# Attention and feed-forward on one core: other places of the row-maximum tiles among the key tiles

## The chip, the cores and the metric

The kernel runs on one core of a Trainium2 chip. The metric is the device time of one execution in microseconds (us). A core has TensorE (PE in the profile, with its weight loads as PEld), VectorE (DVE), ScalarE (ACT), GpSimd (POOL) and SyncE (SP), which here only issues DMAs. Each engine works through its own list of instructions in order.

## The reference

Attention over 8 batches of 8 heads, with 1152 keys of 64 numbers, and queries that are the means of two neighbours (576 of them), followed by a feed-forward layer over the 4608 rows that come out:

```python
q_pool = q.reshape(B, H, S // 2, 2, D).mean(axis=3)
scores = scale * np.matmul(q_pool, k.transpose(0, 1, 3, 2))
scores = scores - np.max(scores, axis=-1, keepdims=True)
attn = np.exp(scores)
attn = attn / (np.sum(attn, axis=-1, keepdims=True) + 1e-09)
out = np.matmul(attn, v)
...
h = x @ w_in
g = h - np.tanh(h)
return g @ w_out
```

## The kernel before

The attention part takes two heads at a time, a *pair*; there are 32 pairs (`n_pair`). The two heads of a pair lie on partitions 0 to 63 and 64 to 127, so their matmuls come in twos. A pair is worked in two halves of 288 queries (`HQ`). In a half, nine *key tiles* of 128 keys follow each other (`scores`): four products of two matmuls each, the query and key parts `hi` and `lo` against each other and one product of `ones_k` with `mb`, which subtracts the row maximum. They go into one PSUM tile `ps`; ScalarE takes the exponential of it into `p_f`. After the nine tiles `pv` multiplies all nine `p_f` with the values into one more `ps` tile (the product with the values), and after a pair's second half `z_sums` adds up the exponentials in the same tile. GpSimd prepares these sums (`z_part`).

The row maxima that `mb` holds have to be there before a pair begins. They are worked out for a later pair in between: `max_part` multiplies 128 queries with 384 keys, the `hi` parts alone, for both heads (two matmuls into one `ps` tile), and VectorE reduces the tile to maxima `mx`. There are 15 such products, called *maxima* here, for a pair (five groups of queries, three of keys). They stand in the second half of the pair two before it and in the first half of the pair just before it. When all 15 are there, `max_rows` reduces `mx` to `nm`, TensorE transposes it (`ps<-ident,nm`), ScalarE and VectorE split it into two parts `mt`, and DMAs bring them into `mb` by way of `m_dram`. The transposition opens a second half.

VectorE also makes `lo` of a coming pair and, in steps spread over the pairs, the split weights of the feed-forward layer (`w_block`, tiles `w`), and in seven of the second halves the reciprocals of a finished batch's sums (`rec`).

All `ps` tiles of the attention come from one pool `ps_a` of four buffers (two PSUM banks each): key tiles, maxima, the transposition, the product with the values. A new tile waits until the last read of the tile that had its buffer is done. Which buffer that is, the framework fixes when the program is built.

The order on every engine is that in which the Python code issues it (`InOrder`). The clock of that order is the unit `u`: a half has `G` = 18 units, a key tile is issued at every second one. `add(u, f, at=...)` puts a step into a table. Of a unit, table `first` runs before the key tile, then `early`, then the key tile, then `at`; `pv` comes at the end of a half's last unit. A maximum's reduction stands in `first` of the unit after the maximum. `spots`, in the loop over the pairs, holds the table and unit of the 15 maxima relative to the pair's own start: -54 opens the second half of the pair two before, -36 the first half of the pair before.

All of it is recorded under line 37 (`InOrder`), so the rows are told apart by their tiles.

Of the kernel before, what the change touches and what calls it, by code (L numbers as in the profile page):

```python
# [43 lines left out]
def kernel(  # L44
# [90 lines left out]
    t, n = chunks.pop()  # L135
# [4 lines left out]
    with ExitStack() as actx:  # L140
# [26 lines left out]
            nc.gpsimd.memset(ones_k[64 * h:64 * h + 2].bitcast(F32), 1.0)  # L167


        at, first, early = {}, {}, {}  # L170

        def banks(dtype=F32):
            return ps_a.tile([P, 2, 512], dtype, name="ps")
# [3 lines left out]
        def add(u, f, *args, at=at):  # L177
            at.setdefault(u, []).append(lambda: f(*args))
# [83 lines left out]
        def scores(w, half, kt, p):  # L262

            ks = slice(SQ + kt * P, SQ + (kt + 1) * P)
            qs = slice(half * HQ, (half + 1) * HQ)
            ps = banks()
            for i, (x, y) in enumerate(((w.hi[:, ks], w.hi[:, qs]), (w.hi[:, ks], w.lo[:, qs]), (w.lo[:, ks], w.hi[:, qs]),
                                        (ones_k, w.mb[:, qs]))):
                for h in range(2):
                    r = slice(64 * h, 64 * h + 64)  # L270
                    pe.matmul(ps[:, h, 0:HQ], x[r], y[r], start=(i == 0), stop=(i == 3))
            act.activation(p, ps[:, :, 0:HQ], AF.Exp, scale=1.0 / 16)
# [12 lines left out]
        def pv(u, hf):  # L285

            w, ps = hf.w, banks()
            hf.o = ps[:, 0]
            for kt in range(KT):
                for h in range(2):  # L290
                    pe.matmul(hf.o[64 * h:64 * h + 64, 0:HQ], w.v[:, h, kt], hf.p[kt][:, h], start=(kt == 0),
                              stop=(kt == KT - 1), tile_position=(0, 64 * h))
            add(u + 1, o_out, w, hf, at=first)
            w.halves.append(hf)
            if hf.n == 1:
                z_sums(u, w, ps[:, 1])
# [95 lines left out]
        for i, blk in enumerate(blocks):  # L392
            u = U * (i - 2) + 5 if i else 23
# [23 lines left out]
        for pi in range(n_pair):  # L417
            u = pi * U
            units = dict(load=-80, query_sums=-62, hi=-55, lo=-37, load_v=-30)
            row, steps = -19, (5, 11)  # L420

            spots = [x for half, us in ((-54, (2, 4, 8, 10, 12, 14, 16)), (-36, (2, 4, 8, 10, 14, 16)))
                     for x in [(early, half)] + [(at, half + i) for i in us]]
            if pi == 0:
                units.update(load=-70, query_sums=-62, hi=-60, lo=-41, load_v=-40)
                spots = [(at, -60 + i) for i in range(15)]
                row, steps = -43, (3, 4)
            if pi == 1:
                units.update(load=-104)
            add(u + units["load"], load, pi)  # L430
            add(u + units["query_sums"], query_sums, pi, dve if pi < 1 else pool)
            for c in range(0, KQ, SQ):
                add(u + units["hi"], hi_part, pi, c, c + SQ)
            add(u + units["lo"], lo_part, pi)
            for i, (when, x) in enumerate(spots):
                add(u + x, max_part, u + x, pi, i // 3, i % 3, at=when)
            add(u + units["load_v"], load_v, pi)
            add(u + row, max_rows, u + row, pi, steps)

        def run(u, at=at):  # L440

            while at.get(u):
                at[u].pop(0)()

        for u in range(min(at), 0):
            run(u, first)
            run(u, early)
            run(u)
        z_groups = {kts[-1]: kts for kts in ((0, 1, 2), (3, 4, 5), (6, 7))}
        for u in range(end + 60):  # L450
            run(u, first)
            run(u, early)
            n, r = divmod(u, G)
            if u < end and r % 2 == 0:
                if r == 0:
                    hf = Half()
                    hf.w, hf.n, hf.p, hf.zs = pairs[n // 2], n % 2, [], []
                hf.p.append(pf.tile([P, 2, HQ], F32, name="p_f"))
                scores(hf.w, hf.n, r // 2, hf.p[-1])
                if r // 2 in z_groups:  # L460
                    add(u + 1, z_part, hf, z_groups[r // 2])
            run(u)
            if u < end and r == G - 1:
                pv(u, hf)
        assert not any(x for t in (at, first, early) for x in t.values())


    wt = ctx.enter_context(tc.tile_pool(name="wt", bufs=1))
# [141 lines left out]
```

## Time and profile before

| | |
|---|---|
| time, median of 3 runs | 1665.53 us (1661.75 to 1668.51) |
| the profiled execution, its own time | 1668.33 us |
| its span in the profile | 1666.5 us |
| PE busy | 1621.7 us (97%) |
| DVE busy | 1322.2 us (79%) |
| ACT busy | 1021.2 us (61%) |
| POOL busy | 939.8 us (56%) |
| chain that ended last, by engine | PE 84%, DVE 13%, ACT 2%, issue 1% |

A row of a timeline names an engine's instructions merged where they are alike: start, time, and how many (x4 is two of a maximum and two of the key tile behind it). TensorE's matmuls overlap, so the starts tell more than the busy times. A wait stands in brackets with the instruction that ended it.

### The profile page before, as it was taken

What the parts mean: (1) busy time and instruction counts of PE and PEld (TensorE: products, weight loads), DVE (VectorE), ACT (ScalarE), POOL (GpSimd) and SP (SyncE); (2) the same over time, 40 slices, a digit from 0 to 9 for tenths busy, and PEclk for the clock granted to TensorE, in tenths of its full rate; (3) what the DMA queues carried; (4) which work ended last, traced back from release to release, by engine and by line L of the source; (5) the groups of instructions that cost most, each with busy time, mean ns of one, the idle gap of its engine ahead of it and who ended that gap; (6) DMA issues with size and microseconds to landing.
All of it is one profiled execution on the core that took longest, in us unless ns stands there. A gap on an engine that the chain in (4) does not pass through costs nothing.

```text
span 1666.5 us, 32223 instructions
## 1 busy us (share of the span) xinstructions
PE 1621.7 (97%) x12576; PEld 1251.9 (75%) x12576; DVE 1322.2 (79%) x1725; ACT 1021.2 (61%) x1865; POOL 939.8 (56%) x694
## 2 busy tenths in 40 slices
PE   5999999999999999999999999999999999999999
PEld 3666776777777677777778787887878787878897
DVE  7888889889888889888657677676767676776886
ACT  2655655656656556556566666566666666665776
POOL 2777878778778778778844243334334332422332
PEclk9999999999999999999999999999999999999999
DMA  3343443443344334335464101101010111010000
GB/s 139 118 136 107 139 136 108 126 134 122 124 128 130 124 115 144 123 106 163 143 242 158 38 26 40 37 14 51 26 51 26 38 39 38 26 37 15 25 27 26
DMA packets 72665, 147.86 MB, mean 89 GB/s; under 512 B 11136, under 2 KB 36672, under 8 KB 72512
## 3 DMA queue, kind: packets, MB, share of 16 engines
q1 hardware_dynamic: 72512, 145.80, 26.8%
q8 instruction: 99, 1.62, 0.4%
q14 instruction: 54, 0.44, 0.1%
HBM read 109.49 MB, written 36.27 MB: 87 GB/s over the span
## 4 chain that ended last, share of the span: by engine, by line
PE 84%; DVE 13%; ACT 2%; issue 1%; DMA 0%; DVEq 0%; ACTq 0%
PE ps L37 37%; PE ps_h L37 24%; PE ps_o L37 23%; DVE w L37 6%; DVE mx L37 6%; DVE nm L37 0%; DVE lo L37 0%; ACT g_s L512 0%; ACT g_m L513 0%; ACT g_s L511 0%; ACT g_u L509 0%; DMA q_n<-in_q_dram 0%; ACT g_hi L520 0%; ACT o_s L539 0%; ACT g_t L510 0%
## 5 line engine op out<-in xcount | busy, mean ns | idle before, releaser
L37 DVE TENSOR_REDUCE mx<-ps 128x2 f32<-128x768 f32 x480 | 434.3, 950 | 74.8 <-PE ps L37 74.7
L37 POOL TENSOR_TENSOR g_lo<-g_s,g_hi 128x512 fp32r<-128x512 f32 (+1 forms) x160 | 189.9, 1187 | 511.5 <-ACT g_hi L520 464.9
L37 ACT ACTIVATE p_f<-ps 128x576 f32<-128x576 f32 x576 | 361.5, 650 | 94.3 <-PE ps L37 79.7
L37 POOL TENSOR_TENSOR z<-p_f 128x576 f32<-128x576 f32 x192 | 279.6, 1456 | 154.7 <-ACT p_f L37 154.7
L37 PE MATMUL ps<-hi 64*128 64x288 f32 (+1 forms) x2112 | 316.9, 352 | 23.7 <-DVE mx L37 13.7
L37 PE MATMUL ps_h<-x,wi 128*128 128x512 f32 (+1 forms) x1440 | 327.2, 377 | 0.0
L37 PE MATMUL ps_o<-wo,g_hi 128*128 128x512 f32 x1008 | 311.6, 390 | 0.0
L37 PEld LDWEIGHTS ps_h<-x,wi 128*128 128x128 f32 x1440 | 260.0, 193 | 53.1
L37 PE MATMUL ps<-p_f,v 128*64 128x288 f32 x2304 | 293.5, 409 | 0.0
L37 PEld LDWEIGHTS ps<-hi 64*128 64x128 f32 x2112 | 194.6, 187 | 89.2 <-DVE mx L37 34.6
L509 ACT ACTIVATE g_u<-ps_h 128x512 f32<-128x512 f32 (+1 forms) x160 | 88.8, 555 | 267.8 <-PE ps_h L37 267.5
L37 PEld LDWEIGHTS ps<-p_f,v 128*64 128x64 f32 x2304 | 159.7, 137 | 113.7 <-ACT p_f L37 12.0
L514 DVE SCALAR_TENSOR_TENSOR ps_w<-g_u,ps_h 128x512 f32<-128x512 f32 (+1 forms) x160 | 102.9, 643 | 178.7 <-ACT g_t L510 177.0
L37 PEld LDWEIGHTS ps_o<-wo,g_hi 128*128 128x128 f32 x1008 | 187.5, 188 | 39.1
L37 POOL TENSOR_TENSOR z<-z,p_f 128x576 f32<-128x576 f32 x128 | 194.0, 1516 | 11.9 <-ACT p_f L37 2.0
L37 PE MATMUL ps_o<-wo,g_lo 128*128 128x512 f32 x504 | 196.3, 389 | 0.0
L37 PE MATMUL ps<-lo,hi 64*128 64x288 f32 x1152 | 171.0, 293 | 0.0
L37 PE MATMUL ps<-hi,lo 64*128 64x288 f32 x1152 | 170.9, 293 | 0.0
L37 PE MATMUL ps<-mb,ones_k 64*128 64x288 f32 x1152 | 170.3, 292 | 0.0
L37 ACT ACTIVATE o_s<-ps 128x288 f32<-128x288 f32 x64 | 26.3, 411 | 230.3 <-PE ps L37 230.3
L519 DVE COPY_PREDICATED g_s<-g_m,g_t 128x512 f32<-128x512 int32 (+1 forms) x160 | 116.2, 726 | 17.1 <-DVE g_s L518 0.9
L517 DVE SCALAR_TENSOR_TENSOR ps_w<-g_s,ps_w 128x512 f32<-128x512 f32 (+1 forms) x160 | 102.9, 643 | 16.6 <-ACT g_m L513 0.5
(68 smaller groups left out, 2398.9 us busy)
## 6 DMA issues: line engine op xcount, KB each, us to landing
q_n<-in_q_dram SPq DMA_DIRECT2D x32, 576.0 KB
kq<-in_k_dram SPq DMA_DIRECT2D x32, 576.0 KB
v<-in_v_dram SPq DMA_DIRECT2D x32, 576.0 KB
x_dram<-o_s SPq DMA_DIRECT2D x32, 288.0 KB
out_dram<-o_s SPq DMA_DIRECT2D x34, 256.0 KB
w_raw<-in_moe_w_in_dram SPq DMA_DIRECT2D x16, 512.0 KB
wi_dram<-w_hl SPq DMA_DIRECT2D x16, 512.0 KB
w_raw<-in_moe_w_out_dram SPq DMA_DIRECT2D x16, 512.0 KB
```

The source lines that it names most:

```text
L37: ins = self.tc.keep_in_program_order(f(*args, **kwargs))
L509: nc.scalar.activation(u, h, AF.Square)
L514: nc.vector.scalar_tensor_tensor(w, u, -P0, h, op0=ALU.add, op1=ALU.mult)
L517: nc.vector.scalar_tensor_tensor(w, s2, P2, w, op0=ALU.add, op1=ALU.mult)
L519: last = nc.vector.copy_predicated(s1, m.bitcast(I32), th).ins
```

## The change

The places of the 15 maxima change. Before, the half at -54 has one maximum in front of its first key tile (table `early`) and others behind key tiles 1, 2, 4, 5, 6, 7 and 8 (units 2, 4, 8, 10, 12, 14, 16); the half at -36 has one in front and six behind tiles 1, 2, 4, 5, 7 and 8. After, no maximum stands in front of a first key tile. The half at -54 has its eight behind tiles 1, 2, 4, 5, 7, and three behind 8, the half at -36 its seven behind 0, 1, 3, 4, 6 and two behind 8. The table `early` is gone. Pair 0's maxima keep their places.

```diff
-            spots = [x for half, us in ((-54, (2, 4, 8, 10, 12, 14, 16)), (-36, (2, 4, 8, 10, 14, 16)))
-                     for x in [(early, half)] + [(at, half + i) for i in us]]
+            spots = [half + i for half, us in ((-54, (2, 4, 8, 10, 14, 16, 16, 16)), (-36, (0, 2, 6, 8, 12, 16, 16))) for i in us]
...
-            for i, (when, x) in enumerate(spots):
-                add(u + x, max_part, u + x, pi, i // 3, i % 3, at=when)
+            for i, x in enumerate(spots):
+                add(u + x, max_part, u + x, pi, i // 3, i % 3)
...
             run(u, first)
-            run(u, early)
```

TensorE at the start of a second half (of a pair in the middle), before. The names are those of the words above, with the buffers' numbers; a maximum has 384 columns, a product of a key tile 288:

```order
L37 MATMUL ps_8029<-ident_60,nm_7994 10x128
L37 MATMUL ps_8033<-hi_7945 128x384 x2
L37 MATMUL ps_8037<-hi_7189 128x288 x2
L37 MATMUL ps_8037<-lo_7190,hi_7189 128x288 x2
L37 MATMUL ps_8037<-hi_7189,lo_7190 128x288 x2
L37 MATMUL ps_8037<-mb0_116,ones_k_118 128x288 x2
L37 MATMUL ps_8052<-hi_7189 128x288 x2
L37 MATMUL ps_8052<-lo_7190,hi_7189 128x288 x2
L37 MATMUL ps_8052<-hi_7189,lo_7190 128x288 x2
L37 MATMUL ps_8052<-mb0_116,ones_k_118 128x288 x2
L37 MATMUL ps_8062<-hi_7945 128x384 x2
```

and after:

```order
L37 MATMUL ps_8029<-ident_60,nm_7994 10x128
L37 MATMUL ps_8034<-hi_7186 128x288 x2
L37 MATMUL ps_8034<-lo_7187,hi_7186 128x288 x2
L37 MATMUL ps_8034<-hi_7186,lo_7187 128x288 x2
L37 MATMUL ps_8034<-mb0_116,ones_k_118 128x288 x2
L37 MATMUL ps_8048<-hi_7186 128x288 x2
L37 MATMUL ps_8048<-lo_7187,hi_7186 128x288 x2
L37 MATMUL ps_8048<-hi_7186,lo_7187 128x288 x2
L37 MATMUL ps_8048<-mb0_116,ones_k_118 128x288 x2
L37 MATMUL ps_8058<-hi_7942 128x384 x2
```

The maximum `ps<-hi 128x384` has left the place between the transposition and the first key tile; the first one now stands behind two key tiles.

TensorE at the end of the same half, the last key tile and what follows it up to the product with the values (`p_f,v`), before:

```order
L37 MATMUL ps_8171<-hi_7189 128x288 x2
L37 MATMUL ps_8171<-lo_7190,hi_7189 128x288 x2
L37 MATMUL ps_8171<-hi_7189,lo_7190 128x288 x2
L37 MATMUL ps_8171<-mb0_116,ones_k_118 128x288 x2
L37 MATMUL ps_8181<-hi_7945 128x384 x2
L37 MATMUL ps_8189<-p_f_8036,v_7532 64x288 x2
```

and after:

```order
L37 MATMUL ps_8163<-hi_7186 128x288 x2
L37 MATMUL ps_8163<-lo_7187,hi_7186 128x288 x2
L37 MATMUL ps_8163<-hi_7186,lo_7187 128x288 x2
L37 MATMUL ps_8163<-mb0_116,ones_k_118 128x288 x2
L37 MATMUL ps_8173<-hi_7942 128x384 x2
L37 MATMUL ps_8176<-hi_7942 128x384 x2
L37 MATMUL ps_8179<-hi_7942 128x384 x2
L37 MATMUL ps_8189<-p_f_8033,v_7531 64x288 x2
```

Three maxima stand between the last key tile and the product with the values, where there was one.

VectorE at the start of the same half, with the reciprocals that seven of the halves have, before:

```order
L37 TENSOR_SCALAR rec_7911<-rec_7911 128x36
L37 RECIPROCAL rec_7911<-rec_7911 128x36
L37 TENSOR_REDUCE mx_7944<-ps_8033 128x2
L37 TENSOR_TENSOR mt_7996<-ps_8029,mt_7996 10x128
L37 TENSOR_REDUCE mx_7944<-ps_8062 128x2
```

and after:

```order
L37 TENSOR_SCALAR rec_7910<-rec_7910 128x36
L37 RECIPROCAL rec_7910<-rec_7910 128x36
L37 TENSOR_TENSOR mt_7996<-ps_8029,mt_7996 10x128
L37 TENSOR_REDUCE mx_7941<-ps_8058 128x2
L37 TENSOR_REDUCE mx_7941<-ps_8074 128x2
```

The first reduction to `mx` stood ahead of `mt`, VectorE's part of the transposed maxima, and now stands behind it. On ScalarE and GpSimd the order of the instructions is the same.

## Rows read from the trace of the kernel before

**Rows 1.** One stretch: us; busy PE, PEld, DVE, ACT, POOL; granted clock, DMA share, GB/s.
```profile
110.00:805.00 695.00, 689.74 (x7663) 497.93 (x7661) 615.97 (x643) 418.37 (x738) 551.66 (x356) 1.00 0.39 127
```

**Rows 2.** Waits, 110 to 805 us: waiting, released by, total us, times, longest.
```profile
PEld ps L37 <- ACT p_f L37: 23.7, 126, 0.5
...
PEld ps L37 <- DVE mx L37: 15.9, 54, 0.8
```

**Rows 3.** Timeline of PE, a turn half: start, us, instruction, count.
```profile
506.42 0.28 PE L37 MATMUL ps<-ident,nm 128*10 128x128 f32 x1
506.62 0.57 PE L37 MATMUL ps<-hi 64*128 64x384 f32 x4
...
508.19 0.63 PE L37 MATMUL ps<-hi 64*128 64x384 f32 x4
...
509.05 0.46 PE L37 MATMUL ps<-hi 64*128 64x384 f32 x4
...
509.74 0.40 PE L37 MATMUL ps<-hi 64*128 64x288 f32 x2
...
512.85 0.51 PE L37 MATMUL ps<-hi 64*128 64x384 f32 x4
...
513.88 0.46 PE L37 MATMUL ps<-p_f,v 128*64 128x288 f32 x2
```

**Rows 4.** Timeline of DVE, the same half and the start of the next.
```profile
507.19 0.94 DVE L37 TENSOR_REDUCE mx<-ps 128x2 f32<-128x768 f32 x1
508.54 0.28 DVE L37 TENSOR_TENSOR mt<-ps,mt 10x128 fp32r<-10x128 f32 x1 [0.41 <-ACT mt L37]
508.75 1.80 DVE L37 TENSOR_REDUCE mx<-ps 128x2 f32<-128x768 f32 x2
510.76 4.42 DVE L37 TENSOR_REDUCE mx<-ps 128x2 f32<-128x768 f32 x5 [0.21 <-PE ps L37]
515.10 3.01 DVE L37 TENSOR_TENSOR lo<-kq,hi 128x1728 fp32r<-128x1728 f32 x1
...
520.96 0.96 DVE L37 TENSOR_REDUCE mx<-ps 128x2 f32<-128x768 f32 x1 [0.97 <-PE ps L37]
```

**Rows 5.** Timeline of ACT, the same half.
```profile
507.71 0.65 ACT L37 ACTIVATE p_f<-ps 128x576 f32<-128x576 f32 x1 [0.77 <-PE ps L37]
508.26 0.25 ACT L37 ACTIVATE mt<-ps 10x128 fp32r<-10x128 f32 x1
...
513.12 1.39 ACT L37 ACTIVATE p_f<-ps 128x576 f32<-128x576 f32 x2 [0.21 <-PE ps L37]
```

**Rows 6.** Timeline of PE, the plain half that follows: its first matmuls, the product.
```profile
520.47 0.58 PE L37 MATMUL ps<-hi 64*128 64x384 f32 x4
...
527.14 0.46 PE L37 MATMUL ps<-p_f,v 128*64 128x288 f32 x2
```

**Rows 7.** Timeline of PE, first key tiles of a half without maxima.
```profile
810.94 0.40 PE L37 MATMUL ps<-hi 64*128 64x288 f32 x2
...
811.58 0.29 PE L37 MATMUL ps<-hi 64*128 64x288 f32 x2
...
812.12 0.29 PE L37 MATMUL ps<-hi 64*128 64x288 f32 x2
```

**Rows 8.** Timeline of ACT, the first exponential there.
```profile
811.87 0.65 ACT L37 ACTIVATE p_f<-ps 128x576 f32<-128x576 f32 x1 [0.61 <-PE ps L37]
```

**Rows 9.** Timeline of PE, a turn half with reciprocals: transposition and product.
```profile
556.91 0.28 PE L37 MATMUL ps<-ident,nm 128*10 128x128 f32 x1
...
564.76 0.46 PE L37 MATMUL ps<-p_f,v 128*64 128x288 f32 x2
```

**Rows 10.** Timeline of PE, the long waits of three early halves.
```profile
75.67 0.58 PE L37 MATMUL ps<-hi 64*128 64x384 f32 x4 [1.83 <-DVE mx L37]
...
90.67 0.40 PE L37 MATMUL ps<-hi 64*128 64x288 f32 x2 [1.10 <-DVE mx L37]
...
102.75 0.58 PE L37 MATMUL ps<-hi 64*128 64x384 f32 x4 [0.84 <-DVE mx L37]
```

More of the change, by code (lines that the diff above doesn't have):

```diff
@@ L167 @@
             nc.gpsimd.memset(ones_k[64 * h:64 * h + 2].bitcast(F32), 1.0)
-        at, first, early = {}, {}, {}
+        at, first = {}, {}
         def banks(dtype=F32):
@@ L420 @@
             row, steps = -19, (5, 11)
-            spots = [x for half, us in ((-54, (2, 4, 8, 10, 12, 14, 16)), (-36, (2, 4, 8, 10, 14, 16)))
-                     for x in [(early, half)] + [(at, half + i) for i in us]]
+            spots = [half + i for half, us in ((-54, (2, 4, 8, 10, 14, 16, 16, 16)), (-36, (0, 2, 6, 8, 12, 16, 16))) for i in us]
             if pi == 0:
                 units.update(load=-70, query_sums=-62, hi=-60, lo=-41, load_v=-40)
-                spots = [(at, -60 + i) for i in range(15)]
+                spots = [-60 + i for i in range(15)]
                 row, steps = -43, (3, 4)
@@ L451 @@
             run(u, first)
-            run(u, early)
             n, r = divmod(u, G)
@@ L464 @@
                 pv(u, hf)
-        assert not any(x for t in (at, first, early) for x in t.values())
+        assert not any(x for t in (at, first) for x in t.values())
     wt = ctx.enter_context(tc.tile_pool(name="wt", bufs=1))
```

## The prediction

> **What bounds the kernel now.** I read the totals by stretch first, then the waits of the stretch in which the change works, and there single halves, instruction by instruction. From 110 to 805 us TensorE is busy for 689.7 of 695 us, at a granted clock of 1.00 [rows 1]. So only TensorE's own waits can give or take time, and they are small: its weight loads waited 23.7 us for exponentials (p_f) and 15.9 us for reductions (mx) [rows 2]. What these cost the totals don't tell; the starts of the instructions do.
>
> A **turn half** is the second half of a pair: it opens with the transposition of the row maxima (ps<-ident,nm) and has eight maxima among nine key tiles, 0 to 8. It takes 7.46 us from the transposition (506.42) to the first product with the values (513.88) [rows 3]. A **plain half**, the first of a pair, has seven and takes 6.67 us, 520.47 to 527.14 [rows 6]. The product with the values and the sums that follow are untouched.
>
> The prices. Key tiles follow each other in 0.53 us (811.58 to 812.12), but a tile that starts cold, first in a half or after a wait, takes 0.64 (810.94 to 811.58) [rows 7]. A maximum and a warm tile take 0.69 (509.05 to 509.74), so the maximum 0.16; where the maximum had waited, the two take 0.86 (508.19 to 509.05) [rows 3]. An exponential lasts 0.65 us and the next instruction of ACT follows 0.55 later (507.71 to 508.26) [rows 5]. It begins 0.93 after a cold tile (810.94 to 811.87) [rows 7, 8] and 0.84 after a warm one: tile 8 stands 0.17 behind the maximum of 512.85, at 513.02, and its exponential at 513.86 (513.12 + 1.39 - 0.65) [rows 3, 5]. A reduction lasts 0.94 and the next follows after 0.87 (five in 4.42) [rows 4]. A tile that waits for a buffer starts 0.05 after the read that frees it (508.75 + 0.94 = 509.69, tile at 509.74 [rows 3, 4]), the product with the values 0.11 after it (513.12 + 0.65 = 513.77, product at 513.88 [rows 3, 5]).
>
> All tiles share four PSUM buffers, and the built program fixes which read each tile waits for. Now reductions pace a turn half: the first runs at 507.19, in time in which VectorE would otherwise wait for the transposed maxima (mt at 508.54), and from 508.75 to 515.10 they run nearly without a gap [rows 4].
>
> **The change, part by part.** No instruction is added or removed. In 30 turn halves and 31 plain ones (the last three halves have no maxima) one maximum leaves the front, and two or three now stand behind tile 8.
>
> *The turn half*, from the transposition as zero. Tile 0 starts at 0.20, as the maximum did (506.42 to 506.62 [rows 3]), but cold, tile 1 at 0.84. Exponential 0 runs from 1.13 to 1.78. The first maximum stands at 1.37. Tile 2 needs exponential 0's buffer: 1.83, where TensorE was free at 1.53, so it has waited 0.3 and is cold. Second maximum 2.47, tiles 3 and 4 2.64 and 3.17, third maximum 3.70. On VectorE the early reduction is gone, and mt comes first. ACT turns the maxima 0.55 after exponential 0 began, at 1.68; VectorE's mt follows 0.28 later (508.26 to 508.54), at 1.96, the first reduction 0.21 after that (508.54 to 508.75 [rows 4, 5]), at 2.17, the second from 3.04 to 3.98. Tile 5 needs the second's buffer: 4.03, where TensorE was free at 3.86. It is cold again: fourth maximum 4.67, tiles 6 and 7 4.83 and 5.36, fifth maximum 5.89, tile 8 6.05. The three maxima behind it are covered, since the product with the values now takes tile 8's buffer and so waits for the last exponential, where it waited for the one before: 6.05 + 0.84 + 0.65 + 0.11 = 7.65; I take 7.66. Against 7.46 that is **+0.20 us, 30 times, +6.0**. What the change gains, that VectorE drains three reductions under the 6.6 us of product and sums (513.88 to 520.47 [rows 3, 6]), is there, but the latencies of the first and of the last exponential come out into the open.
> Bounds: with no wait but that for exponential 0, tile 8 stands 0.17 + 0.11 earlier: -0.08. If the two waits for reductions (tile 5's, and the last maximum's, which takes the fifth's buffer) each pass another 0.1 on: +0.40. I stay with the walk, whose prices are all from such halves.
>
> *The plain half*, from its first matmul as zero. Tile 0 at 0, its exponential 0.93 to 1.58; first maximum 0.64, tile 1 0.80, second maximum 1.37. Tile 2 waits for exponential 0 until 1.63. Tile 3 2.27, third maximum 2.80, tile 4 2.97, fourth 3.54; tile 5 waits 0.1 for exponential 3: 3.79. Tile 6 4.43, fifth 4.96, tile 7 5.13, tile 8 and two maxima until 6.5; the product waits for exponential 7 (5.95 to 6.60): 6.71. Against 6.67 that is **+0.04, 31 times, +1.2**. Bounds: -0.10 without tile 5's wait and with the product right behind the maxima, +0.15 if the last maximum's wait for a reduction ends last.
>
> *The reciprocals.* In seven turn halves VectorE also adds and inverts the sums of a finished batch ahead of the first reduction, and the half takes 7.85 us (556.91 to 564.76 [rows 9]) instead of 7.46. After the change mt stands behind them, for which VectorE has to wait anyway (0.41 us [rows 4]), so they are hidden: 7 x 0.39 = **-2.7**. This cover is thin: the plain half's last reductions end, by the walk, some 0.4 us later than now, and with them the steps on the weights (w) that stand ahead of mt. They reach 1.2 us after the transposition (now 507.19 - 506.42 = 0.8 at the latest [rows 3, 4]), 0.7 ahead of mt, 0.1 with the reciprocal. Uncovered, it gives back these 2.7 us and no more.
>
> *The start.* In three halves of the first 110 us VectorE comes late from more such steps, and TensorE waits 1.83, 1.10 and 0.84 us [rows 10]. Now it has up to two more tiles and a maximum to do, 1.2 us, before it meets a late reduction, and no more can be saved than these waits exceed the usual 0.3. I estimate 1.0, 0.5 and 0.5: **-2.0** (bounds -3.3 and 0).
>
> *Other queues.* ACT's and GpSimd's orders stay as they are, and no DMA of SP is moved. lo and w behind the turn half's reductions start some 0.8 us later; VectorE idles 0.97 us before the plain half's first reduction [rows 4], and that now comes later too, so nobody waits for them. Were that cover gone, the price would be in the plain half's +0.15.
>
> **Sum:** 6.0 + 1.2 - 2.7 - 2.0 = +2.5 us. The profiled execution took 1668.3 us, 0.2% over the median of 1665.5, so a difference this small may stand on the median: **1668.0 us**. A measurement of this kernel can tell about 0.5% (8.3 us) from no change; this is less.
>
> **A rule against it.** TensorE waited 1.83 us in one place, and waits of tenths stand in every half, at a granted clock of 1.00 [rows 1, 10]. The Trainium skill, page "TensorE: Matmul & The Clock Gate", section "A second HAM failure mode: psum-queue depth-cycling", says that short idle times between groups of matmuls, while the PSUM buffers are cycled, can make the clock swing between its levels and cost throughput. By that rule more waits per half speak against the change; the trace of before shows nothing of it. As a mechanism here, nine key tiles at half the clock add 9 x 0.53 = 4.8 us to each half that it hits, 290 us if all 61.
>
> **Rivals.** *Slower: the late first reduction.* In the turn half everything from tile 5 on hangs on mt, now ahead of all reductions, and on exponential 0 before it. With +0.40 and +0.15, and the reciprocals then uncovered: 30 x 0.40 + 31 x 0.15 - 2.0 = +14.7, 1680 us. It decides from +0.39 in a turn half on (30 x 0.39 + 1.2 - 4.7 = 8.2). For it: each of these waits ends right where a tile needs it. Against it: VectorE is free 0.7 us before mt. *Faster: the waits vanish.* With the lower bounds of both halves and of the start, 30 x (-0.08) - 31 x 0.10 - 2.7 - 3.3 = -11.5, 1654 us. For it: VectorE gets work under the product with the values. Against it: tile 2 must wait for exponential 0 whatever else happens. *The change does nothing:* the built program shows the maxima moved, so only the effect can be nil, which is the forecast. *The clock*, as above.
>
> **How the numbers follow.** Forecast, within 0.5%: 0.68. Slower by the late reduction 0.19, by the clock 0.01. Faster 0.12. The range takes in most of the faster case, down to 1656, and goes up to 1678, which leaves out the clock and about half of the slower case: below 0.2 in all. Faster 0.12, same 0.68, slower 0.20.
>
> **What would show it.** From the transposition to the values 7.66 us in a turn half, and 6.71 in a plain one; a wait for p_f ahead of the third key tile in both, a wait for mx ahead of the sixth in the turn half; the values' product released by the last exponential there; two to three reductions under it; halves with a reciprocal as long as the others. I am wrong if a turn half takes less than 7.4 or more than 7.85 us, or if the product or the sums, held here at their length, change.

## The result

| | before | after |
|---|---|---|
| time, median of 15 runs each | 1667.31 us (1661.75 to 1668.51) | 1670.91 us (1667.90 to 1672.67) |
| ratio to before, with its 95% interval | | 1.0023 [1.0015, 1.0031] |
| span of the profiled execution | 1666.5 us | 1669.7 us |
| turn half, transposition to the product with the values (median of 20) | 7.47 us | 7.71 us |
| turn half with reciprocals (median of 7) | 7.86 us | 7.71 us |
| plain half, first matmul to the product (median of 28) | 6.665 us | 6.70 us |

No change by the bound of 0.5%, and a small loss that the interval separates from zero: 0.0023 x 1665.5 = 3.8 us (2.5 to 5.2). The halves in this table and below are those that start behind 105 us, so that the three early ones of [rows 10] stand by themselves.

The page of after, its head, the busy times of TensorE and VectorE, and the chain that ended last by engine:

```profile
span 1669.7 us, 32193 instructions
...
PE 1629.6 (98%) x12576; PEld 1251.4 (75%) x12576; DVE 1287.9 (77%) x1725; ACT 1018.2 (61%) x1865; POOL 887.4 (53%) x694
...
PE 94%; ACT 3%; DVE 2%; issue 0%; DMA 0%; ACTq 0%; DVEq 0%
```

The same instructions, and VectorE is off the chain: it held 13% of it before. The stretch 110 to 805 us of after, with the columns of [rows 1]:

```profile
110.00:805.00 695.00, 691.40 (x7607) 493.84 (x7605) 580.00 (x640) 412.74 (x733) 498.50 (x353) 1.00 0.39 126
```

The granted clock is 1.00 as in [rows 1]. VectorE is 36 us less busy and GpSimd 53 us, with nearly the same instructions in the stretch; the last section comes back to that. The waits of the stretch, which answer to [rows 2]:

```profile
PEld ps L37 <- ACT p_f L37: 37.1, 163, 0.7
...
DVE mt L37 <- ACT mt L37: 19.3, 27, 0.9
PEld ps L37 <- DVE mx L37: 10.8, 54, 0.2
```

TensorE's waits have gone over from reductions (15.9 to 10.8 us) to exponentials (23.7 to 37.1 us), as a kernel shows in which the latencies of ScalarE lie open. For `mt` VectorE now waits in all 27 turn halves (8.4 us in 21 of them before).

TensorE in a turn half of after, which answers to [rows 3]. A row of [rows 3] takes in a maximum and the key tile behind it; here key tiles 0, 2, 5 and 8 (288 columns), the last maximum (384) and the product are shown apart:

```profile
507.26 0.28 PE L37 MATMUL ps<-ident,nm 128*10 128x128 f32 x1
507.47 0.40 PE L37 MATMUL ps<-hi 64*128 64x288 f32 x2
...
509.10 0.41 PE L37 MATMUL ps<-hi 64*128 64x288 f32 x2
...
511.29 0.40 PE L37 MATMUL ps<-hi 64*128 64x288 f32 x2
...
513.38 0.35 PE L37 MATMUL ps<-hi 64*128 64x288 f32 x2
...
514.60 0.45 PE L37 MATMUL ps<-hi 64*128 64x384 f32 x2
514.97 0.46 PE L37 MATMUL ps<-p_f,v 128*64 128x288 f32 x2
```

VectorE in the same half ([rows 4]):

```profile
509.23 0.28 DVE L37 TENSOR_TENSOR mt<-ps,mt 10x128 fp32r<-10x128 f32 x1 [0.83 <-ACT mt L37]
509.43 1.80 DVE L37 TENSOR_REDUCE mx<-ps 128x2 f32<-128x768 f32 x2
511.44 1.82 DVE L37 TENSOR_REDUCE mx<-ps 128x2 f32<-128x768 f32 x2 [0.21 <-PE ps L37]
513.58 3.55 DVE L37 TENSOR_REDUCE mx<-ps 128x2 f32<-128x768 f32 x4 [0.32 <-PE ps L37]
517.05 2.96 DVE L37 TENSOR_TENSOR lo<-kq,hi 128x1728 fp32r<-128x1728 f32 x1
```

ScalarE in the same half ([rows 5]):

```profile
508.40 0.65 ACT L37 ACTIVATE p_f<-ps 128x576 f32<-128x576 f32 x1 [0.61 <-PE ps L37]
508.94 0.25 ACT L37 ACTIVATE mt<-ps 10x128 fp32r<-10x128 f32 x1
...
512.19 2.69 ACT L37 ACTIVATE p_f<-ps 128x576 f32<-128x576 f32 x4 [0.21 <-PE ps L37]
```

Three places are to be seen. Tile 2 starts at 509.10, where exponential 0 has ended at 509.05 (508.40 + 0.65). Tile 5 starts at 511.29, behind the second reduction, which ended at 511.23 (509.43 + 1.80). The product with the values starts at 514.97, behind the last exponential, which ended at 514.88 (512.19 + 2.69), but also 0.37 behind the last maximum. That one starts at 514.60, 0.06 behind the end of a reduction (the first of the four from 513.58; 514.54). Which of the two holds the product these rows don't decide; e3 below bears on it. Before, the first reduction ran 0.77 us behind the transposition [rows 3, 4], now it runs 2.17 behind it. Two of the four reductions from 513.58 on start under the product.

The plain half that follows, first matmul, third key tile and product ([rows 6]), a turn half with reciprocals ([rows 9]), with VectorE in it, and TensorE's one wait that is left of [rows 10]:

```profile
521.56 0.40 PE L37 MATMUL ps<-hi 64*128 64x288 f32 x2
...
523.19 0.40 PE L37 MATMUL ps<-hi 64*128 64x288 f32 x2
...
528.26 0.46 PE L37 MATMUL ps<-p_f,v 128*64 128x288 f32 x2
```

```profile
456.26 0.28 PE L37 MATMUL ps<-ident,nm 128*10 128x128 f32 x1
...
463.97 0.71 PE L37 MATMUL ps<-p_f,v 128*64 128x288 f32 x4
```

```profile
457.49 0.38 DVE L37 RECIPROCAL rec<-rec 128x36 f32<-128x36 f32 x1
458.23 0.28 DVE L37 TENSOR_TENSOR mt<-ps,mt 10x128 fp32r<-10x128 f32 x1 [0.35 <-ACT mt L37]
```

```profile
75.61 0.57 PE L37 MATMUL ps<-hi 64*128 64x384 f32 x4 [0.48 <-DVE mt L37]
```

### The profile page after: what moved, and what is told of

It is laid out like the page before. It is cut to its first block, busy times and chain, and to the rows that moved or that the text cites. A ratio compares the mean times of both kernels' runs of the same rounds, so it can differ in the third digit from the quotient of the medians.

```text
span 1669.7 us, 32193 instructions
## 1 busy us (share of the span) xinstructions
PE 1629.6 (98%) x12576; PEld 1251.4 (75%) x12576; DVE 1287.9 (77%) x1725; ACT 1018.2 (61%) x1865; POOL 887.4 (53%) x694
## 4 chain that ended last, share of the span: by engine, by line
PE 94%; ACT 3%; DVE 2%; issue 0%; DMA 0%; ACTq 0%; DVEq 0%
PE ps L37 47%; PE ps_h L37 24%; PE ps_o L37 23%; DVE mx L37 1%; ACT p_f L37 1%; DVE w L37 0%; ACT g_s L508 0%; ACT g_m L510 0%; ACT g_s L509 0%; ACT g_u L506 0%; DMA q_n<-in_q_dram 0%; ACT g_hi L517 0%; ACT o_s L536 0%; ACT g_t L507 0%; ACT hi L37 0%
## 5 line engine op out<-in xcount | busy, mean ns | idle before, releaser
L37 POOL TENSOR_TENSOR z<-p_f 128x576 f32<-128x576 f32 x192 | 287.4, 1497 | 196.3 <-ACT p_f L37 194.9
L37 PE MATMUL ps<-hi 64*128 64x288 f32 (+1 forms) x2112 | 328.5, 353 | 19.0 <-ACT hi L37 8.5
L37 PEld LDWEIGHTS ps<-hi 64*128 64x128 f32 x2112 | 198.2, 187 | 93.4 <-ACT p_f L37 29.6
L37 POOL TENSOR_TENSOR z<-z,p_f 128x576 f32<-128x576 f32 x128 | 183.4, 1433 | 10.0
```

The source lines that it names most:

```text
L37: ins = self.tc.keep_in_program_order(f(*args, **kwargs))
```

## The experiments

All are the kernel before with one thing changed (e9 with two). The table gives the lengths in us as above, and the start of VectorE's first reduction counted from the transposition (median of the 20 turn halves without reciprocals); ratios are to the kernel before, with 95% intervals. The expectations count a turn half from its first matmul behind the transposition, which is 0.20 us less.

| kernel | turn half | with reciprocals | plain half | first reduction | ratio |
|---|---|---|---|---|---|
| before | 7.47 | 7.86 | 6.665 | 0.78 | |
| after | 7.71 | 7.71 | 6.70 | 2.17 | 1.0023 [1.0015, 1.0031] |
| e1: turn half as after, plain half as before | 7.71 | 7.71 | 6.66 | 2.17 | 1.0011 [1.0003, 1.0020] |
| e2: plain half as after, turn half as before | 7.68 | 8.14 | 6.70 | 1.05 | 1.0044 [1.0031, 1.0057] |
| e3: no front in the turn half, one behind | 7.86 | 7.86 | 6.66 | 2.17 | 1.0037 [1.0026, 1.0049] |
| e7: no front in the turn half, two behind | 7.80 | 7.80 | 6.66 | 2.17 | 1.0025 [1.0014, 1.0037] |
| e4: front kept in the turn half, three behind | 7.59 | 7.98 | 6.665 | 0.79 | 1.0022 [1.0014, 1.0031] |
| e6: front kept, its reduction behind `mt` | 8.33 | 8.34 | 6.66 | 2.35 | 1.0131 [1.0115, 1.0147] |
| e5: reciprocals behind the first reduction | 7.47 | 7.86 | 6.66 | 0.78 | 1.0011 [1.0002, 1.0019] |
| e8: reciprocals behind the turn half | 7.47 | 7.47 | 6.66 | 0.78 | 0.9983 [0.9973, 0.9993] |
| e9: e8, and 7 maxima in the turn half, 8 in the plain one | 7.145 | 7.145 | 7.00 | 0.78 | 0.9979 [0.9969, 0.9990] |

**One half at a time.** e1 takes the new places in the turn half alone, e2 in the plain half alone.

```diff
 e1
+            spots = [(at, -52), (at, -50), (at, -46), (at, -44), (at, -40), (at, -38), (at, -38), (at, -38),
+                     (early, -36), (at, -34), (at, -32), (at, -28), (at, -26), (at, -22), (at, -20)]
 e2
+            spots = [(early, -54), (at, -52), (at, -50), (at, -46), (at, -44), (at, -42), (at, -40), (at, -38),
+                     (at, -36), (at, -34), (at, -30), (at, -28), (at, -24), (at, -20), (at, -20)]
```

> Turn half as in the changed kernel (none in front, three behind the last tile), plain half as before. Both theories of the turn half (the missing head start of VectorE, or the three maxima behind) expect it at 7.50 us from its first matmul (7.27 before, 7.50 after) and the plain half at 6.67, seven halves with reciprocals no longer than the others: 30 x 0.235 - 2.6 - some 1.5 in the two late turn halves of the start = +3 us, ratio 1.002. If the cost sat in the plain half: ratio 1.000 or below.

> Plain half as in the changed kernel, turn half as before, its front maximum kept. The theory that VectorE's steps are queued one behind the other: the plain half's last reductions end some 0.4 us later, so do the weight steps behind them, and the turn half's early reduction, now uncovered, starts 0.4 later: turn half 7.6 to 7.7, plain half 6.70, those with reciprocals 8.1: 30 x 0.38 + 31 x 0.035 = +12.5 us, ratio 1.0075. The rival, that each half pays for its own order alone: turn half 7.27, +1 us, ratio 1.0007.

Each half takes in its experiment the length that it has in after: the turn half of e1 7.71 (7.51 as the expectations count), the plain half of e2 6.70. But e2 also lengthens the turn half, in which nothing was moved, from 7.47 to 7.68 (7.48 as they count), and those with reciprocals to 8.14. VectorE at the head of such a half of e2 (the transposition starts at 512.42):

```profile
511.40 1.44 DVE L37 TENSOR_SCALAR w<-w 128x512 int32<-128x512 int32 x1
512.87 0.69 DVE L37 SCALAR_TENSOR_TENSOR w<-w_raw,w 128x512 f32<-128x512 uint16 x1
513.48 0.95 DVE L37 TENSOR_REDUCE mx<-ps 128x2 f32<-128x768 f32 x1
```

The plain half's later reductions push the weight steps (`w`) on, and the front maximum's reduction, which stands behind them, starts 1.06 instead of 0.77 us behind the transposition. The theory had the direction right and the size too large: it expected the reduction 0.4 later, 7.6 to 7.7 and a ratio of 1.0075, and the runs show 0.29, 7.48 and 1.0044. In after the same delay falls into VectorE's wait for `mt`: 0.83 us there, 1.10 in e1, whose plain half is the old one. So the two parts don't add up: alone, the plain half's new order costs 0.21 + 0.035 a pair, beside the turn half's new order only 0.035. After is cheaper than its parts, 1.0023 against 1.0011 and 1.0044.

**What the lost front costs, and what the places behind the last tile give.** In the turn half alone: e3 gives up the front and keeps one maximum behind tile 8, e7 has two there, e1 three; e4 keeps the front and has three behind.

```diff
 e3
+            spots = [(at, -52), (at, -50), (at, -48), (at, -46), (at, -44), (at, -42), (at, -40), (at, -38),
 e7
+            spots = [(at, -52), (at, -50), (at, -48), (at, -46), (at, -44), (at, -40), (at, -38), (at, -38),
 e4
+            spots = [(early, -54), (at, -52), (at, -50), (at, -46), (at, -42), (at, -38), (at, -38), (at, -38),
...
+                     (early, -36), (at, -34), (at, -32), (at, -28), (at, -26), (at, -22), (at, -20)]
```

> Turn half without a maximum in front, one behind each tile from the second on, so one behind the last, as before; plain half as before. Theory of the lost head start: the cost of the change is all here, turn half 7.45 to 7.65, ratio 1.002 to 1.004. Rival, that the maxima behind the last tile cost and the front doesn't matter: turn half 7.27 or less, and with the reciprocals hidden -3 us, ratio 0.998.

> Turn half with its front maximum kept and three maxima behind the last tile (those behind tiles 5 and 7 moved there); plain half as before. Rival (the three behind cost, since the product then waits for the last exponential): turn half 7.5, +7 us, ratio 1.004, reciprocals not hidden. Theory of the lost head start in its pure form: turn half 7.27 or less, ratio 1.000. A walk with the prices of the rows of before gives 7.4 to 7.5, the same cost by another road: then the two are not additive, and each alone costs what both together cost.

> Turn half without a maximum in front and with two behind the last key tile (the changed kernel has three there, the earlier experiment without a front place had one); plain half as before. Theory (each maximum behind the last key tile gives back its part of what the lost head start costs, since its reduction lies under the product): the turn half lies between 7.65 (one behind) and 7.505 (three behind), at 7.55 to 7.60, ratio 1.0020 to 1.0030 beside 1.0037 and 1.0011. Rival (only the third one gives back, because it moves the last wait to the maximum before it): 7.65 as with one, ratio 1.0035; or rival (two give it all back, the third costs a wait): 7.48 or less, ratio 1.001 or less.

As the expectations count, the turn halves are 7.65 (e3), 7.59 (e7), 7.51 (e1) and 7.385 (e4). Giving up the front costs 7.86 - 7.47 = 0.39 us a turn half; the second maximum behind tile 8 gives 0.06 of it back, the third 0.09, and 0.24 is left, which is after. That each of them gives back its part is what the theory of e7 asked for. With the front kept, three behind cost 0.12 (7.59). So the same three places are a gain in one order and a loss in the other, and the two changes don't add up to 0.24 (0.39 + 0.12 = 0.51). VectorE shows why. In e3, behind its `mt` (transposition at 509.42), and then, by order of time, ScalarE's exponential 7, TensorE's last maximum and the product:

```profile
511.38 0.28 DVE L37 TENSOR_TENSOR mt<-ps,mt 10x128 fp32r<-10x128 f32 x1 [1.10 <-ACT mt L37]
511.59 6.99 DVE L37 TENSOR_REDUCE mx<-ps 128x2 f32<-128x768 f32 x8
```

```profile
516.24 0.65 ACT L37 ACTIVATE p_f<-ps 128x576 f32<-128x576 f32 x1 [0.21 <-PE ps L37]
516.90 0.44 PE L37 MATMUL ps<-hi 64*128 64x384 f32 x2
517.27 0.46 PE L37 MATMUL ps<-p_f,v 128*64 128x288 f32 x2
```

and in e4 (transposition at 508.80, product at 516.39):

```profile
509.59 0.94 DVE L37 TENSOR_REDUCE mx<-ps 128x2 f32<-128x768 f32 x1
...
513.16 0.96 DVE L37 TENSOR_REDUCE mx<-ps 128x2 f32<-128x768 f32 x1 [0.21 <-PE ps L37]
514.55 0.96 DVE L37 TENSOR_REDUCE mx<-ps 128x2 f32<-128x768 f32 x1 [0.43 <-PE ps L37]
515.79 2.69 DVE L37 TENSOR_REDUCE mx<-ps 128x2 f32<-128x768 f32 x3 [0.28 <-PE ps L37]
```

In e3 eight reductions run without a gap: VectorE began them 1.4 us later than in the kernel before and paces the half to its end. The last maximum starts at 516.90, behind the sixth reduction, which by the pitch of the eight ended at 516.85 (511.59 + 5 x 0.865 + 0.94). There it helps to let reductions slip under the product. In e4 VectorE has its head start and waits for TensorE three times. TensorE still waits for reductions in it (16.0 us in 54 waits from 110 to 805 us, as before), but not at the end of the half, and what three maxima behind tile 8 do there is to leave the last exponential in the open (ScalarE's last one ends at 516.33 by 513.90 + 2.43, and the product starts at 516.39).

**The head start by itself.** In e6 the front maximum stays where it is on TensorE, and only its reduction is issued two steps later, behind `mt`.

```diff
-            add(u + 1, lambda: dve.tensor_reduce(w.mx[:, t, :, c], ps[:, :, 0:CH], axis=AX.X, op=ALU.max), at=first)
+            late = u % U == G and 0 <= u < end
+            add(u + (3 if late else 1), lambda: dve.tensor_reduce(w.mx[:, t, :, c], ps[:, :, 0:CH], axis=AX.X, op=ALU.max), at=first)
```

> The kernel before with one edit: in the turn half the reduction of the front maximum is issued two steps later, so that on VectorE it stands behind its part of mt, which waits for ScalarE's part; the maximum itself stays in front of the first key tile on TensorE, and all the others keep their places. VectorE's order at the head of the turn half is then that of the changed kernel, TensorE's that of the kernel before. Theory (the front place is worth the head start of its reduction, and holds a buffer pair until then): the turn half loses more than by giving up the front place alone, 0.6 to 0.9 instead of 0.385 to a turn half, +18 to +26 us, ratio 1.011 to 1.016; the first reduction begins at 2.0 or later behind the transposition instead of 0.77. Rival (a maximum whose reduction is late costs the same whether it stands in front or not): +0.24 to +0.39, +7 to +12 us, ratio 1.003 to 1.007.

8.33 us, 0.86 more than before, and ratio 1.0131: as the theory had it, and more than twice what giving up the front place costs. TensorE and VectorE in such a half, from the transposition on:

```profile
517.99 0.28 PE L37 MATMUL ps<-ident,nm 128*10 128x128 f32 x1
...
520.00 0.86 PE L37 MATMUL ps<-hi 64*128 64x384 f32 x4 [0.30 <-ACT p_f L37]
```

```profile
520.13 0.28 DVE L37 TENSOR_TENSOR mt<-ps,mt 10x128 fp32r<-10x128 f32 x1 [1.29 <-ACT mt L37]
520.34 2.67 DVE L37 TENSOR_REDUCE mx<-ps 128x2 f32<-128x768 f32 x3
```

The second maximum starts 2.01 us behind the transposition, in the kernel before 1.77 [rows 3], and waits for an exponential instead of a reduction; the first reduction starts at 2.35 instead of 0.77. The front place on TensorE is still paid for, and nothing comes of it: it is worth only the reduction that it lets VectorE do early. The change gives up both together, which is the cheap way.

**The reciprocals.** They cost 0.39 us in each of seven halves (0.46 in e2) as long as a reduction stands ahead of `mt`, and nothing in any kernel where none does: after, e1, e3 and e7 without the front, and e6 with it. e5 moves them two steps on, between the first reduction and `mt`, e8 moves them behind the whole turn half:

```diff
 e5
-                    add(u + 17, lambda: reciprocals(dve, *tot[0]))
-                    add(u + 20, lambda: spread(sp, *tot.pop(0)))
+                    add(u + 19, lambda: reciprocals(dve, *tot[0]))
+                    add(u + 22, lambda: spread(sp, *tot.pop(0)))
 e8
+                    add(u + 36, lambda: reciprocals(dve, *tot[0]))
+                    add(u + 39, lambda: spread(sp, *tot.pop(0)))
```

> The kernel before with one edit: the four reciprocals of a batch are issued two steps later, behind the turn half's first reduction and ahead of the VectorE part of mt, and their spreading DMA two steps later too; no maximum moves. Theory (the reciprocals cost time in the kernel before only because they stand ahead of the first reduction, on the way to the second maximum's buffer; in the changed kernel they stand under the wait for mt, where they cost nothing): the seven turn halves with reciprocals go from about 7.65 to 7.3 to 7.4, the other turn halves stay 7.27, in all -2.0 to -2.7 us, ratio about 0.9985. Rival (VectorE is short of time in that half wherever they stand): 7.6 to 7.65 as before, ratio 1.000.

The theory fell: 7.86 as before. VectorE and GpSimd of e5 in such a half (transposition at 556.48):

```profile
558.12 0.60 DVE L37 TENSOR_SCALAR rec<-rec 128x36 f32<-128x36 f32 x1
...
559.05 0.22 DVE L37 TENSOR_TENSOR mt<-ps,mt 10x128 fp32r<-10x128 f32 x1
```

```profile
557.41 1.27 POOL L37 TENSOR_TENSOR w<-w,w 128x512 f32<-128x512 f32 x1 [0.63 <-DVE w L37]
```

The scaling of the sums takes 0.60 us here and ends at 558.72, 0.04 behind GpSimd's product (557.41 + 1.27 = 558.68); it is so in all seven halves (0.60 to 0.62), while in every other kernel it takes 0.17 or 0.18. It waits for GpSimd, and `mt` and all reductions behind it wait with it. So the mistake was to take the gap ahead of `mt` for free time: VectorE is idle there, but what this instruction needs is not. The timed ratio of e5, 1.0011, is more than its profile shows (span 1662.9 us, halves as before). The profile is of the shortest of its twelve executions, 1664.64 us; what the longer ones do stays open.

> The kernel before with one edit: the four reciprocals of a batch stand behind the turn half, behind lo and the two weight steps that follow it on VectorE, where VectorE then waits for the next half's first maximum (in the kernel before it is idle 1.09 us there, 570.75 to 571.84) and GpSimd is idle too (from 570.01 to 573.72). The run with them two steps later showed their scaling taking 0.60 instead of 0.17 us and ending 0.04 behind GpSimd's weight product in each of the seven halves. Theory (it is the place that costs: at the head of the turn half they are in the way of the first reduction or of mt, whichever they precede, and under GpSimd's product the scaling waits for it): six of the seven turn halves with reciprocals become as long as the others, 7.27, the last 7.5, the scaling takes 0.17 again, in all -2.3 to -2.7 us, ratio about 0.9985. Rival (these halves are longer for another reason, such as the DMAs of the batch's sums): 7.6 to 7.65 as before, ratio 1.000 or above.

Here the theory holds: all turn halves take 7.47, the scaling 0.18, and the time is 1663.34 us against 1665.70, ratio 0.9983. VectorE behind a turn half of e8:

```profile
569.02 1.95 DVE L37 TENSOR_SCALAR w<-w 128x512 f32<-128x512 f32 x2
570.88 0.18 DVE L37 TENSOR_SCALAR rec<-rec 128x36 f32<-128x36 f32 x1
...
571.97 0.96 DVE L37 TENSOR_REDUCE mx<-ps 128x2 f32<-128x768 f32 x1 [0.50 <-PE ps L37]
```

0.50 us of the idle time are left, so it is covered. Two plain halves of e8 take 6.92 instead of 6.66, for a reason that stays open. This version beats both kernels, by a little.

**One maximum from one half to the other.** e9 is e8 with front places in both halves, seven maxima in the turn half and eight in the plain one.

```diff
-            spots = [x for half, us in ((-54, (2, 4, 8, 10, 12, 14, 16)), (-36, (2, 4, 8, 10, 14, 16)))
+            spots = [x for half, us in ((-54, (2, 4, 8, 10, 14, 16)), (-36, (2, 4, 8, 10, 12, 14, 16)))
```

> The kernel with the reciprocals behind the turn half, and besides one maximum moved from the turn half to the plain half: front maxima kept in both halves, 7 in the turn half and 8 in the plain half. Theory (a half's length goes by how many maxima have to be reduced ahead of its last wait, and the front place pays in both halves; the eighth maximum costs about 0.5 to 0.6 in whichever half it stands, a little less where there is no mt): turn half 6.70 to 6.80, plain half 7.10 to 7.20, sum of both 13.85 to 13.95 instead of 13.93, ratio beside the run with the reciprocals alone 0.998 to 1.000. Rival (the weight steps of the plain half stand behind a longer row of reductions and reach into the turn half, as they did when the plain half alone had its new places): turn half 7.0 or more, sum 14.1 or more, ratio 1.002 or more.

Turn half 7.145 (6.94 as the expectation counts), plain half 7.00: the sum is that of e8 (14.145 against 14.13), and so is the time (1662.51 and 1663.34 us, with overlapping intervals). That the sum would stay came true; the sizes did not: an eighth maximum costs 0.33 in either half, not 0.5 to 0.6, and neither half has the better place for it.

## Why the prediction was right

The time came out within 3 us of the forecast, on the side of no change (1670.91 against 1668.0; 1.8 us of that lie in the kernel before, whose median of 15 runs is 1667.31 and not the 1665.53 that the forecast stood on), for the reasons given, and single steps can be held against the rows.

*The turn half.* +0.24 measured, +0.20 forecast. From the transposition at 507.26 as zero: exponential 0 at 1.14 (walked 1.13), tile 2 at 1.84 (1.83), `mt` at 1.97 (1.96), first reduction at 2.17 (2.17), tile 5 at 4.03 (4.03), tile 8 at 6.12 (6.05), the product at 7.71 (7.66). The 0.05 that are missing arise between tiles 5 and 8: tile 8 is 0.07 late, and from there on the walk holds, since the last exponential begins 0.85 us after it (512.19 + 2.69 - 0.65 = 514.23; walked 0.84). One step is not shown as forecast: the walk had the three maxima covered and the product released by the last exponential alone, but it is as far behind the last maximum (0.37) as in e3, where no exponential holds it, so that both end together. What the runs add is how the 0.24 is made up: 0.39 lost with the front and 0.15 won back by the places behind tile 8.

*The plain half.* +0.035 against +0.04, 6.70 against 6.71; its third key tile starts at 1.63 (523.19 - 521.56), as walked.

*The reciprocals.* Hidden, as forecast: the half of 456.26 takes 7.71. VectorE still waits 0.35 for `mt` with them, 0.83 without; the walk gave 0.1 and 0.7, so the cover was thicker than thought. One of the seven halves, at 558 us, takes 7.99 and one, at 763, 7.79; before, the one at 760 took 8.10. So the seven give back 6 x 0.39 + 0.63 less 0.28 and 0.08, 2.6 us in all; why a few halves are longer is not known.

*The start.* The three early halves took 8.97, 7.80 and 7.97 us from their first matmul to the product, and take 8.32, 6.91 and 7.51. Beside the usual +0.24, +0.035 and +0.24 that is 0.89 + 0.93 + 0.70 = 2.5 us saved, where 2.0 was estimated. It is the least certain term: in e8, which is the kernel before up to 152 us, the first of the three took 10.34 instead of 8.97. One profile of either kernel can't give this term to better than 1.4 us.

*The sum.* 30 x 0.235 + 31 x 0.035 - 2.6 - 2.5 = +3.0 us. In the traces the product of the last half with maxima starts at 806.22 before and at 809.35 after, +3.13. The timed difference is 3.8 us (2.5 to 5.2), the forecast was +2.5. Product and sums, held at their length, have kept it: 4.52 us from a plain half's product to the next transposition and 6.59 from a turn half's to the next plain half in both kernels.

*Where the walk does not hold.* The same walk for the experiments, with the buffers as each program fixes them (its steps are not shown here), gives turn halves (counted from the first matmul) of 7.44 for e1 (measured 7.51), 7.62 for e7 (7.59), 7.48 for e4 (7.385), 8.17 for e6 (8.13), but 7.45 for e3 (7.65) and 7.65 for e2 (7.48). So its error is up to 0.1 in most orders and 0.2 in two; over 30 halves that is 3 to 6 us, as much as the whole difference here. That the sum came out this close owes something to luck. In e3 what is missing lies at the end of the half. The prices put its last maximum at 7.51 behind the transposition (2.17 + 5 x 0.87 + 0.94 + 0.05), and it starts at 7.48. With 0.16 behind it, the price of a maximum that has not waited, that makes 7.67, about the walk's 7.65 (7.45 from the first matmul); but this one has waited, and the product comes 0.37 behind it, in e7 too. No exponential holds it there: number 7 ended at 516.89 and number 8 was still running. The prediction's own row of a maximum that had waited (0.86 with its tile, so 0.33) would have given 7.84 for e3, against 7.86 measured. Whether the walk of e2 errs in the same way is not shown.

*The rivals.* The slower case needed +0.39 in a turn half. e3 is that case: a first reduction as late as in after, without the three places behind tile 8, gives +0.39, and even there the reciprocals stay hidden and the ratio is 1.0037. So the mechanism of that rival was real, and what decides against it is what the places behind tile 8 take off. The faster case would have needed tile 2 not to wait, and it waits for exponential 0 in the rows. As to the clock, it is 1.00 from 110 to 805 us before and after, while waits of a few tenths stand in each half, and 1.00 in e3 and e6 with their longer halves as well; the rule against it, of the Trainium skill, page "TensorE: Matmul & The Clock Gate", section "A second HAM failure mode: psum-queue depth-cycling", is not borne out by this kernel.

## What to carry to other kernels

Walk the critical stage by the starts of instructions, with two prices for each (behind a wait, and back to back): it told the sign and size to 0.1 or 0.2 us a half, which the totals of waits did not. An instruction that an engine does while it would wait for another one anyway is worth a head start to everything behind it (here 0.39 us a half), and whether work moved under a later stage gains or loses depends on which engine paces the end of the stage: reckon the parts together, since here neither the two halves nor the two changes in the turn half added up. Before something is put into idle time of VectorE, look at what GpSimd does there.

## What was not expected of the hardware

In the rows of this kernel VectorE and GpSimd shut each other out for whole instructions where both work in SBUF. Groups of GpSimd and of VectorE from 110 to 805 us, by form (count, busy us, mean ns, idle time before), first of the kernel before:

```profile
L37 POOL TENSOR_TENSOR w_hl<-w,w_hl 128x512 fp32r<-128x512 f32 x28 | 83.7, 2990 | 0.0
...
L37 DVE TENSOR_SCALAR w<-w 128x512 f32<-128x512 f32 x28 | 41.8, 1492 | 0.0
```

then of after:

```profile
L37 POOL TENSOR_TENSOR w_hl<-w,w_hl 128x512 fp32r<-128x512 f32 x28 | 37.4, 1334 | 0.0
...
L37 DVE TENSOR_SCALAR w<-w 128x512 f32<-128x512 f32 x28 | 12.7, 453 | 0.0
```

The same instructions on the same shapes take 2.99 or 1.33 us, and 1.49 or 0.45. GpSimd's weight product of one pair, with the sum ahead of it before, and then after:

```profile
514.90 1.39 POOL L37 TENSOR_TENSOR z<-p_f 128x576 f32<-128x576 f32 x1
516.26 2.98 POOL L37 TENSOR_TENSOR w_hl<-w,w_hl 128x512 fp32r<-128x512 f32 x1
```

```profile
516.92 1.28 POOL L37 TENSOR_TENSOR w_hl<-w,w_hl 128x512 fp32r<-128x512 f32 x1
```

In the kernel before VectorE's `lo` (515.10 to 518.11 [rows 4]) starts ahead of it, and it ends 1.13 us behind `lo`, at 519.24. In after `lo` starts at 517.05, 0.13 behind it, and it takes its 1.28 alone. Whoever comes second waits, and its record shows the wait as time of its own. `lo` itself comes second in both kernels: it ends 1.82 us behind GpSimd's sum before (514.90 + 1.39 = 516.29) and 1.81 behind the product in after (518.20), whatever its record says (3.01 and 2.96 us). From 110 to 805 us its end lies 1.81 or 1.82 us behind that of the GpSimd instruction it started under, in all 27 cases of either kernel. The Trainium skill, page "SBUF — State Buffer", section "🔬 SBUF: two separate sides", calls the port pair that the two share an exclusive lock that is held for the whole instruction; the rows agree, and so does e5, whose scaling ended 0.04 us behind GpSimd in seven halves of seven. The reductions, which read PSUM, keep their 0.95 us beside GpSimd in both kernels. So the busy time of VectorE that the change takes off (36 us in this stretch, and 53 us of GpSimd's) is no work saved, and as neither engine paced these places it bought nothing.
